# Attention of a fused attention, expert and feed-forward kernel: order from a list scheduler, scores by row halves, V stationary by column halves

## The chip, the cores and the metric

One core of a Trainium2 chip runs the whole program. Each core has five engines with queues of their own, worked off in order: TensorE (matmuls and transposes), VectorE, ScalarE, GpSimd and SyncE, which here issues DMA transfers. The metric is the device time of one execution in microseconds (us), lower is better.

## What is computed

Three layers follow one another; the change is in the first and in the gate of the second. All data are fp32.

```python
# attention: q, k, v are (2, 8, 768, 64), n_global = 8, n_local = 96
rel = pos[:, None] - pos[None, :]
keep = (pos[None, :] < n_global) | ((rel >= 0) & (rel < n_local))
scores = q @ k.T / sqrt(64) - slopes[h] * dist      # dist: |rel|, n_local for far global keys
a = softmax(where(keep, scores, -1e9)); x = a @ v   # x: 1536 tokens of 512
# experts: 8 of them, 512 -> 1024 -> 512, capacity 384
expert = argmax(x @ w_gate); gate_w = softmax(x @ w_gate)[expert]
y = gate_w * (relu(x @ w1[expert]) @ w2[expert])
# feed-forward: 512 -> 2048 -> 512
out = softplus(y @ w_in) @ w_out
```

## The kernel before

`fast_path` works through three stages. **Attention** has 12 tiles: 2 batches with 6 blocks of 128 queries. A query sees its own block of 128 keys, the 96 keys before it and 8 global keys, so a full tile has 232 columns of scores per head, and the first block of a batch (tiles 0 and 6) has 128. **The experts** take the tokens sorted by expert, **the feed-forward layer** takes them in three chunks of 512 and 16 blocks of the hidden layer, 48 steps, each with a first and a second group of products. Both of these keep the weights as a high and a low part, and so take three products where attention takes one.

Order is set by the program text: the framework is told to keep the order in which the instructions are written, and adds the waits. Attention is a loop over n = 0 to 103 (L978), where n is the tile times 8 plus the head. Step n issues the exponential of head n-2 (`expo`, L751), the biased scores of head n-1 (`biased`, L740), the scores of head n (`scores`, L731), the transposes of the probabilities of head n-4 (`transp`, L755) and, at every other n, the products with V of heads n-7 and n-6 (`pv`, L774). Preparation of the next tile (`prep`, L680, transposes q and k), loads, and the routing of the tile before (`route`, L809) are hung on chosen heads.

In `scores` the contraction is over 64 channels, but the matmul uses all 128 rows: k is kept with two heads stacked, and q in two zero-padded copies, `qpad`, of which each has one of the two heads. In `pv` the transposed probabilities are the weights (128 columns) and V moves (64 columns and a column of ones, whose product is the sum of the probabilities). `pv` then divides by the sum (L794 to L796). `route` transposes the tokens x in step 0 (L815), multiplies by the gate's weights and finds the expert in step 1 (L823 to L834), and in step 2 takes the gate's probability, the token's rank in its expert, its slot, the weighted token `xg` (on GpSimd, L864) and scatters it to `xs_d` (L805).

Expert 0 doesn't wait for the last two tiles' scatters: `first_base` (L944) multiplies the rows that are already in `xs_d` by the identity, and `first_add` (L954) adds those of the last two tiles by a selection matrix `here`. Beside attention, `conv_step` (L502) turns pieces of w_in and w_out from double to single precision for the last stage, with one piece a call (64 in all), and goes on later; `pump` (L458) loads weights and splits them into parts (L436, L448) once the pieces of a block are converted. `bank` hands out the eight banks of PSUM by four tags: A has 2, B 3, C 2, D 1.

The lines that set the pace in a step of the loop:

```python
nc.tensor.matmul(ps[:, :w], tr[i][h % 2][:, h // 2, :], kwin[t % 2][:, h // 2, c0:], start=True, stop=True)
...
nc.tensor.matmul(ps[:, o:o + D + 1], pT[:w, 2 * (h % 2) + j, :], vsrc[:w, h, :], start=(j == 0), stop=(j == nb - 1))
```

Of the kernel before, what the change touches and what calls it, by code (L numbers as in the profile page):

```python
# [22 lines left out]
P = 128  # L23
# [65 lines left out]
def strict_upper(nc, pool, name, room=None, ints=None, **kw):  # L89

    t = fill_iota(nc, room or pool, [P, P], [[-1, P]], 0, 1, name + "_rel", ints, **kw)
    tri = pool.tile([P, P], BF16, name=name)
    nc.vector.tensor_scalar(tri, t, 0.0, None, op0=ALU.is_lt)
    return tri

# [216 lines left out]
def fast_path(ctx, tc, q, k, v, n_global, n_local, w_gate, w1, w2, cap, w_in, w_out, out, const):  # L312
# [86 lines left out]
    NRAW = 4  # L399
    rawq = deque()  # L400
# [149 lines left out]
    vt = [ac.tile([P, H, D + 1], F32, name=f"vt{i}") for i in range(3)]  # L550
    vp = [ac.tile([P, H, D + 1], F32, name=f"vp{i}") for i in range(2)]
# [19 lines left out]
    def load_v(i):  # L571
        if i >= len(tiles):
            return
        b, t = tiles[i]
        s0 = t * P
        rotated(vt[i % 3][:, :, 0:D], v, b, s0)
# [43 lines left out]
    for t_ in vt + vp:  # L620
        nc.gpsimd.memset(t_[:, :, D:D + 1], 1.0)
    qpad = [[ac.tile([P, H // 2, P], F32, name=f"qpad{i}{j}") for j in range(2)] for i in range(2)]
    for qa, qb in qpad:
        nc.gpsimd.memset(qa[D:], 0.0)
        nc.gpsimd.memset(qb[:D], 0.0)
# [19 lines left out]
    wg = const.tile([P, NC, E], F32, name="wg")  # L645
    nc.sync.dma_start(wg, w_gate.rearrange("(c p) e -> p c e", p=P))
# [21 lines left out]
    def make_bias1(h):  # L668
        if h == 0:
# [8 lines left out]
    tr = {}  # L678

    def prep(i, step):  # L680

        if i >= len(tiles):
            return
        b, t = tiles[i]
        src = ld[i][step].rearrange("p h d -> p (h d)")
        ps = bank("A", "ps_prep")
        for j in range(H // 2):
            nc.tensor.transpose(ps[:, j * P:(j + 1) * P], src[:, j * P:(j + 1) * P], ident)
        psv = ps.rearrange("p (j c) -> p j c", j=H // 2)
        if step == 0:  # L690

            tr[i] = qpad[i % 2]
            nc.vector.tensor_copy(tr[i][0][:D], psv[:D])
            nc.vector.tensor_copy(tr[i][1][D:], psv[D:])
        else:
            nc.scalar.copy(kwin[t % 2][:, :, PRE:], psv)
            del ld[i]

    def prep_first():

        tr[0] = qpad[0]
        for g in range(2):
# [9 lines left out]
            nc.scalar.copy(tr[0][0][:D, js, :], psv[:D, 0])  # L712
            nc.scalar.copy(tr[0][1][D:, js, :], psv[D:, 0])
# [15 lines left out]
    sps, pt_, ptp, pts, pvs, xts = {}, {}, {}, {}, {}, {}  # L729

    def scores(n):  # L731
        i, h = divmod(n, H)
        b, t = tiles[i]
        c0 = 0 if t else PRE
        w = WIN - c0
        ps = bank("B", "ps_s")
        nc.tensor.matmul(ps[:, :w], tr[i][h % 2][:, h // 2, :], kwin[t % 2][:, h // 2, c0:], start=True, stop=True)  # L737
        sps[n] = ps

    def biased(n):  # L740
        i, h = divmod(n, H)
        t = tiles[i][1]
        w = WIN if t else P
        ps = sps.pop(n)
        s_sb = a3.tile([P, WIN], F32, name="s_sb", bufs=5)
        nc.vector.tensor_tensor_reduce(s_sb[:, :w], in0=ps[:, :w], in1=(bias1 if t else bias0)[:, h, :],  # L746
                                       scale=-(D ** -0.5), scalar=3.0e38, op0=ALU.add, op1=ALU.min,
                                       accum_out=negm[:, n:n + 1])
        pt_[n] = s_sb

    def expo(n):  # L751
        w = WIN if tiles[n // H][1] else P
        nc.scalar.activation(pt_[n][:, :w], pt_[n][:, :w], AF.Exp, bias=negm[:, n:n + 1], scale=-1.0)  # L753

    def transp(n):  # L755
        i, h = divmod(n, H)
        nb = 2 if tiles[i][1] else 1
        if h % 2 == 0:
            ptp[n // 2] = bank("C", "ps_pt")
        ps = ptp[n // 2]  # L760
        s_sb = pt_.pop(n)
        o = (h % 2) * 2 * P
        for j in range(nb):
            nc.tensor.transpose(ps[:, o + j * P:o + (j + 1) * P], s_sb[:, j * PRE:j * PRE + P], ident)
        if h % 2:
            ptp.pop(n // 2)
            pT = a3.tile([P, 4, P], F32, name="pT", bufs=2)
            c = nb * P
            src = ps.rearrange("p (a c) -> p a c", a=2)[:, :, :c]
            dst = pT.rearrange("p (a j) c -> p a (j c)", a=2)[:, :, :c]  # L770
            nc.scalar.copy(dst, src)
            pts[n // 2] = pT

    def pv(n):  # L774
        i, h = divmod(n, H)
        b, t = tiles[i]
        nb = 2 if t else 1
        pT = pts[n // 2]
        if h % 4 == 0:
            pvs[n // 4] = bank("D", "ps_pv")  # L780
        ps = pvs[n // 4]
        o = (h % 4) * (D + 1)
        for j in range(nb):
            vsrc, w = (vt[i % 3], P) if j == nb - 1 else (vp[t % 2], PRE)
            nc.tensor.matmul(ps[:, o:o + D + 1], pT[:w, 2 * (h % 2) + j, :], vsrc[:w, h, :], start=(j == 0), stop=(j == nb - 1))
        if h % 2:
            pts.pop(n // 2)
        if h % 4 == 3:
            pvs.pop(n // 4)
            if h == 3:  # L790
                xts[i] = a2.tile([P, H, D], F32, name="x", bufs=3)
            pv_ = ps[:, :4 * (D + 1)].rearrange("p (a d) -> p a d", a=4)
            rs = a2.tile([P, 4], F32, name="rs")
            nc.vector.tensor_scalar(rs, pv_[:, :, D], 1.0e-9, None, op0=ALU.add)  # L794
            nc.vector.reciprocal(rs, rs)
            nc.vector.tensor_tensor(xts[i][:, h - 3:h + 1, :], pv_[:, :, 0:D],  # L796
                                    rs.unsqueeze(2).to_broadcast([P, 4, D]), op=ALU.mult)

    rt = {}
    sc_q = deque()  # L800

    def scatter_x():
        if sc_q:
            sl, xg = sc_q.popleft()
            nc.gpsimd.indirect_dma_start(  # L805
                out=xs_d, out_offset=bass.IndirectOffsetOnAxis(ap=sl, axis=0), in_=xg, in_offset=None,
                bounds_check=NSLOT - 1, oob_is_err=False)

    def route(i, step):  # L809
        x = xts[i]  # L810
        xf = x.rearrange("p h d -> p (h d)")
        if step == 0:
            ps = bank("A", "ps_xT")
            for c in range(NC):
                nc.tensor.transpose(ps[:, c * P:(c + 1) * P], xf[:, c * P:(c + 1) * P], ident)  # L815
            xT = a2.tile([P, NC, P], F32, name="xTr", bufs=1)
            nc.scalar.copy(xT, ps.rearrange("p (c t) -> p c t", c=NC))
            rt[i] = xT
        elif step == 1:
            xT = rt.pop(i)  # L820
            ps = bank("A", "ps_lg")
            for c in range(NC):
                nc.tensor.matmul(ps[:, :E], xT[:, c, :], wg[:, c, :], start=(c == 0), stop=(c == NC - 1))  # L823
            lg = a2.tile([P, E], F32, name="lg")
            nc.vector.tensor_copy(lg, ps[:, :E])
            mx8 = a2.tile([P, 8], F32, name="mx8")
            nc.vector.max(mx8, lg)
            ix8 = a2.tile([P, 8], U32, name="ix8")
            nc.vector.max_index(ix8, mx8, lg)
            nc.vector.tensor_copy(eall[:, i:i + 1], ix8[:, 0:1])  # L830
# [530 lines left out]
```

## Time and profile before

| | |
|---|---|
| median of the runs (598.76, 599.19 and a disturbed one) | 599.19 us |
| the profiled execution, its own time | 600.73 us |
| span of the profiled execution | 598.9 us |
| TensorE busy in the span | 583.5 us (97%), 3446 matmuls |
| VectorE, ScalarE, GpSimd busy | 348.0, 277.9, 107.3 us |
| mean granted clock of TensorE | 0.989 |
| moved by DMA | 91.85 MB, 153 GB/s |

A profile shows one execution. The span runs from its first to its last instruction. An engine is busy while one of its instructions runs; for TensorE the matmuls overlap, so that a row's duration is longer than the distance to the next one's start. In a row of the timeline stand the start, the duration, the engine, the line of the kernel, the operation, the tile written and the tiles read, the shape, and how many instructions the row merges; a bracket at its end tells how long the engine was idle before it and for whom. [...]

### The profile page before, as it was taken

The numbers are of one execution on the slowest core, as the hardware profiler recorded it, in microseconds if no ns is written. First come the engines' busy times: TensorE is split into PE (matmuls) and PEld (weight loads), VectorE is DVE, ScalarE is ACT, GpSimd is POOL, SyncE is SP. The second block draws the span as 40 slices with busy tenths as digits, with TensorE's granted clock in tenths as the row PEclk, the third lists the DMA queues.
The fourth block names the chain that finished last, engine by engine and source line by source line (L and its number), as shares of the span: only waits on it lengthen the run. The fifth ranks groups of instructions, "written<-read, shape, count | busy, mean of one in ns | idle before, by whom it ended". The sixth has DMA issues, their size and how long they took to land. (4 is left out here: it accounts for less than half of the span.)

```text
span 598.9 us, 9968 instructions
## 1 busy us (share of the span) xinstructions
PE 583.5 (97%) x3446; PEld 523.7 (87%) x3446; DVE 348.0 (58%) x1012; ACT 277.9 (46%) x599; POOL 107.3 (18%) x138
## 2 busy tenths in 40 slices
PE   5999999999999999999999999999999999999995
PEld 4899989999999999999999788888888888888874
DVE  7666888865477883313558774555586433432451
ACT  3566676762565653323444544434553333333340
POOL 3213263321000000000235411120052000200201
PEclk9999999996999999999999999999999999999999
DMA  8857578951797888997963465645202000100101
GB/s 161 219 156 193 139 195 225 286 205 37 251 295 227 257 282 304 379 378 240 323 215 99 122 106 99 108 77 149 81 18 90 0 1 1 53 19 0 71 20 56
DMA packets 90815, 91.85 MB, mean 153 GB/s; under 512 B 43189, under 2 KB 61645, under 8 KB 90757
## 3 DMA queue, kind: packets, MB, share of 16 engines
q1 hardware_dynamic: 82117, 73.30, 42.9%
q10 hardware_dynamic: 6336, 11.54, 6.0%
q0 software_dynamic: 2304, 6.30, 2.9%
q8 instruction: 29, 0.48, 0.4%
q14 instruction: 29, 0.24, 0.2%
HBM read 71.71 MB, written 19.41 MB: 152 GB/s over the span
## 5 line engine op out<-in xcount | busy, mean ns | idle before, releaser
L1236 DVE SCALAR_TENSOR_TENSOR sa<-ps_m,sa 128x512 f32<-128x512 f32 x48 | 33.2, 691 | 112.4 <-ACT sa L1235 112.4
L1233 ACT ACTIVATE sa<-ps_m 128x512 f32<-128x512 f32 x48 | 28.7, 598 | 135.6 <-PE ps_m L1126 135.6
L1124 PE MATMUL ps_m<-zh,w1s 128*128 128x512 f32 x192 | 75.3, 392 | 1.2 <-DVE sa L1236 1.1
L1125 PE MATMUL ps_m<-zl,w1s 128*128 128x512 f32 x192 | 74.8, 390 | 0.0
L1124 PE MATMUL ps_o<-w2s,g 128*128 128x512 f32 x192 | 74.8, 390 | 0.0
L1126 PE MATMUL ps_o<-w2s,g 128*128 128x512 f32 x192 | 74.8, 390 | 0.0
L1126 PE MATMUL ps_m<-zh,w1s 128*128 128x512 f32 x192 | 74.7, 389 | 0.0
L1125 PE MATMUL ps_o<-w2s,g 128*128 128x512 f32 x192 | 74.7, 389 | 0.0
L436 POOL TENSOR_TENSOR w1s<-raw,w1s 128x512 fp32r<-128x512 f32 x16 | 23.2, 1469 | 213.7 <-ACT w1s L448 213.7
L753 ACT ACTIVATE s_sb<-s_sb,negm 128x232 f32<-128x232 f32 (+1 forms) x96 | 44.8, 473 | 35.5 <-DVE negm L746 35.2
L1175 PE MATMUL ps_y<-h,w 128*128 128x232 f32 (+4 forms) x320 | 59.1, 328 | 0.0
L1148 PE MATMUL ps_h<-xT,w 128*128 128x232 f32 (+4 forms) x320 | 58.8, 328 | 0.0
L737 PE MATMUL ps_s<-kwin,qpad 128*128 128x232 f32 (+1 forms) x192 | 56.4, 382 | 1.7 <-DVE negm L746 1.7
L1148 PEld LDWEIGHTS ps_h<-xT,w 128*128 128x128 f32 x320 | 52.9, 190 | 0.7 <-ACT xT L1103 0.2
L1175 PEld LDWEIGHTS ps_y<-h,w 128*128 128x128 f32 x320 | 52.3, 190 | 0.5
L1124 PEld LDWEIGHTS ps_m<-zh,w1s 128*128 128x128 f32 x192 | 36.0, 188 | 10.0 <-DVE sa L1236 2.5
L1126 PEld LDWEIGHTS ps_o<-w2s,g 128*128 128x128 f32 x192 | 36.0, 188 | 7.9 <-DVE g L1244 0.4
L1124 PEld LDWEIGHTS ps_o<-w2s,g 128*128 128x128 f32 x192 | 36.1, 188 | 7.8 <-DVE g L1243 0.3
L1126 PEld LDWEIGHTS ps_m<-zh,w1s 128*128 128x128 f32 x192 | 36.1, 188 | 7.5
L1125 PEld LDWEIGHTS ps_m<-zl,w1s 128*128 128x128 f32 x192 | 36.0, 188 | 7.4 <-DVE zl L1183 0.2
L1125 PEld LDWEIGHTS ps_o<-w2s,g 128*128 128x128 f32 x192 | 36.1, 188 | 7.4
L1157 ACT ACTIVATE h<-ps_h 128x232 f32<-128x232 f32 (+4 forms) x40 | 13.3, 332 | 58.9 <-PE ps_h L1148 56.3
(208 smaller groups left out, 1238.9 us busy)
## 6 DMA issues: line engine op xcount, KB each, us to landing
w<-in_moe_w_dram SPq DMA_DIRECT2D x20, 1024.0 KB, 8.9
raw<-in_moe_w_dram SPq DMA_DIRECT2D x24, 512.0 KB, 4.8
cr<-in_moe_w_in_dram ACTq DMA_DIRECT2D x24, 256.0 KB, 4.4
cr<-in_moe_w_out_dram ACTq DMA_DIRECT2D x20, 256.0 KB, 4.6
xs_d<-early SPq DMA_DIRECT2D x18, 256.0 KB, 3.7
wi_d<-ct SPq DMA_DIRECT2D x32, 128.0 KB, 5.4
wo_d<-ct SPq DMA_DIRECT2D x32, 128.0 KB, 4.5
raw<-wi_d SPq DMA_DIRECT2D x8, 512.0 KB, 5.0
```

The lines of the kernel that those rows point to most:

```text
L436: eng.tensor_tensor(lo, raw, f32(hi), op=ALU.subtract)
L737: nc.tensor.matmul(ps[:, :w], tr[i][h % 2][:, h // 2, :], kwin[t % 2][:, h // 2, c0:], start=True, stop=True)
L753: nc.scalar.activation(pt_[n][:, :w], pt_[n][:, :w], AF.Exp, bias=negm[:, n:n + 1], scale=-1.0)
L1124: nc.tensor.matmul(ps, hi_l, hi_r, start=first, stop=False)
L1125: nc.tensor.matmul(ps, hi_l, lo_r, start=False, stop=False)
L1126: nc.tensor.matmul(ps, lo_l, hi_r, start=False, stop=last)
L1148: nc.tensor.matmul(ps, w[:, c, js], x[:, c, :], start=c == 0, stop=c == NC - 1)
L1157: nc.scalar.activation(h[:, :n], ps, AF.Relu)
L1175: nc.tensor.matmul(ys[ui, d], w[:, j, sl], h, start=f == 0, stop=f == NFE - 1)
L1233: nc.scalar.activation(a, ps, AF.Abs)
L1236: nc.vector.scalar_tensor_tensor(a, in0=ps, scalar=0.0, in1=a, op0=ALU.max, op1=ALU.add)
```

## The change

The loop over n goes. Attention's steps become jobs, each with an engine or a choice of two (`either`), a cost, the jobs it comes after, and buffers that it takes and gives back; `arrange` places them one by one, always the one that can start first, and at equal times the one with the smaller rank (its tile plus a number from a table). The steps are then issued in this order. The costs and ranks are constants of the program, and nothing is decided on the chip.

The steps change too. `scores` takes a tile's eight heads as one job, in 64-row matmuls whose neighbours use rows 0 to 63 and 64 to 127 and different banks; `qpad` becomes one `qT`. `expo` sums the probabilities itself. `transp`, the copies of q and k and that of the outputs may be evicted by ScalarE or VectorE. In `pv` V is the weight, on 64 columns, for two heads on columns 0 to 63 and 64 to 127, so the output comes out transposed and undivided. The gate multiplies it as it is by `wg`, spread over 16 columns for each pair of heads, and `choose` divides the 64 products by the heads' sums and adds them up. The tokens are transposed behind the gate (`rows`) and weighted by VectorE (`weighted`), where GpSimd did it before. Conversion has one call in each of tiles 3 to 10, where tiles 5 to 10 had two.

```diff
+def arrange(jobs, sizes, free):
...
+            for e, c in x.cost.items():
+                s = max(t, free[e])
+                key = (max(s, free[e] + SLACK) + (LEAN if e == "DVE" and len(x.cost) > 1 else 0.0), x.rank, s + c)
+                if best is None or key < best[0]:
+                    best = (key, s, e, x)
...
+    "B": -2.6, "C": -1.84, "CH": 10.69, "CL": 12.72, "CNT": 9.95, "CV": -15.21, "DUP": 13.9, "E": -0.74, "FA":
...
+    NS, NPT, NOT = 8, 6, 2
...
-    for qa, qb in qpad:
-        nc.gpsimd.memset(qa[D:], 0.0)
-        nc.gpsimd.memset(qb[:D], 0.0)
+    qT = [ac.tile([P, H // 2, P], F32, name=f"qT{i}") for i in range(2)]
+    wg = const.tile([P, NC, 2 * E], F32, name="wg")
...
+    def place(h):
+        return h // 4 * 2 + h % 2, h // 2 % 2 * (2 * P)
+
+    def scores(i):
...
+        for h in range(H):
+            j, o = place(h)
+            if o == 0:
+                sps[i, j] = bank("ABBB"[j], "ps_s")
+            r = slice(h % 2 * D, (h % 2 + 1) * D)
+            nc.tensor.matmul(sps[i, j][:, o:o + w], qT[i % 2][r, h // 2, :], kwin[t % 2][r, h // 2, c0:],
+                             start=True, stop=True)
...
+        nc.scalar.activation(s_sb, s_sb, AF.Exp, bias=negm[:, n:n + 1], scale=-1.0, accum_out=dens[i][:, h:h + 1])
...
+        for c in range(2 * g, 2 * g + 2):
+            for j in range(nb):
+                vsrc, w = (vt[i % 3], P) if j == nb - 1 else (vp[t % 2], PRE)
+                for a in range(2):
+                    nc.tensor.matmul(pvs[i][a * D:(a + 1) * D, c * P:(c + 1) * P], vsrc[:w, 2 * c + a, :],
+                                     pts[i, 2 * c + a][:w, j, :], start=(j == 0), stop=(j == nb - 1))
+
+    def keep_o(e, i):
+        ots[i] = a2.tile([P, NC, P], F32, name="oT", bufs=NOT)
+        evict(e, ots[i], pvs.pop(i).rearrange("p (c t) -> p c t", c=NC))
...
+        nc.vector.tensor_tensor(lgh, rt.pop((i, "lg"))[:, :H * E].rearrange("p (h e) -> p h e", h=H),
+                                dens[i].unsqueeze(2).to_broadcast([P, H, E]), op=ALU.mult)
+        lg = a2.tile([P, E], F32, name="lg")
+        nc.vector.tensor_reduce(lg, lgh.rearrange("p h e -> p e h"), axis=AX.X, op=ALU.add)
...
+        nc.vector.tensor_tensor(xg, psin.pop(i).rearrange("p (h d) -> p h d", h=H),
+                                dens.pop(i).unsqueeze(2).to_broadcast([P, H, D]), op=ALU.mult)
...
-    for n in range(NH + 8):
-        i, h = divmod(n, H)
-        if 0 <= n - 2 < NH:
-            expo(n - 2)
...
+        job(("S", i), {"PE": 2.0 if t else 1.3}, lambda e, i=i: scores(i),
+            ([("Q", i), ("K", i)] if i else []) + ([("DUP", i - 1)] if t else []),
+            take=[(("A", "B", "B", "B")[j], ("S", i, j), 0.4 * j) for j in range(4)], lag=0.25)
...
+        if 3 <= i < N:
+            job(("CV", i), {"DVE": 1.05}, lambda e: conv_step(1), [("B", i, H - 1)])
...
+    for _, e, x in arrange(jobs, sizes, {"PE": 7.2, "DVE": 7.6, "ACT": 8.0, "POOL": 8.0, "SP": 6.0}):
+        x.run(e)
```

How the change moves instructions is shown at two places of TensorE's queue; lines are those of each kernel's own program, and xN merges equal instructions. The first is the middle of attention, in a full tile. Before, one head's scores (`ps_s`), another's transposes (`ps_pt`) and the products with V (`ps_pv`) alternate; `ps_prep` is k transposed, `ps_rk` the ranks:

```order
L688 MATMUL ps_prep<-ident,kr 128x128 x4
L737 MATMUL ps_s<-kwin_131,qpad_163 128x232
L764 MATMUL ps_pt<-ident,s_sb 128x128 x2
L841 LDWEIGHTS tri
L841 MATMUL ps_rk<-ohb,tri 128x8
L842 LDWEIGHTS ones
L842 MATMUL ps_rk<-acc,ones 128x8
L737 MATMUL ps_s<-kwin_131,qpad_164 128x232
L764 MATMUL ps_pt<-ident,s_sb 128x128 x2
L785 MATMUL ps_pv<-vp_128,pT 128x65
L785 MATMUL ps_pv<-vt_127,pT 128x65
```

After, the same place in a full tile; `ps_x` is the tokens transposed behind the gate, `ps_lg` the gate's products of the tile before:

```order
L797 MATMUL ps_s<-kwin_130,qT_156 128x232 x8
L863 MATMUL ps_lg<-wg,oT 128x16 x4
L919 MATMUL ps_x<-ident,oT 128x128 x4
L849 MATMUL ps_pv<-pT,vp_129 64x128 x2
L849 MATMUL ps_pv<-pT,vt_126 64x128 x2
L849 MATMUL ps_pv<-pT,vp_129 64x128 x2
L849 MATMUL ps_pv<-pT,vt_126 64x128 x2
L830 MATMUL ps_pt<-ident,s_sb 128x128 x8
L748 MATMUL ps_prep<-ident,kr 128x128 x4
L748 MATMUL ps_prep<-ident,qr 128x128 x4
```

The scores of a tile have moved together into one block of eight at its head, the products with V into groups of eight on 64 rows of output, and the transposes between them into larger runs.

The second place is the end of attention. Before, the base of expert 0's tokens (`ps_x` from `xr`) stands behind the ranks of the tile before the last, on either side of the last tile's token transposes:

```order
L841 LDWEIGHTS tri
L841 MATMUL ps_rk<-ohb,tri 128x8
...
L951 MATMUL ps_x_2202<-ident,xr_2092 128x128
L951 MATMUL ps_x_2202<-ident,xr_2092 128x104
...
L815 MATMUL ps_xT<-ident,x 128x128 x4
L951 MATMUL ps_x_2214<-ident,xr_2092 128x128
L951 MATMUL ps_x_2214<-ident,xr_2092 128x104
...
L823 MATMUL ps_lg<-wg,xTr 128x8 x4
```

After, in the same stretch:

```order
L863 MATMUL ps_lg<-wg,oT 128x16 x4
L1015 MATMUL ps_x_2078<-ident,xr_2017 128x128
L1015 MATMUL ps_x_2078<-ident,xr_2017 128x104
...
L889 LDWEIGHTS tri
L889 MATMUL ps_rk<-ohb,tri 128x8
...
L1015 MATMUL ps_x_2088<-ident,xr_2017 128x128
L1015 MATMUL ps_x_2088<-ident,xr_2017 128x104
...
L919 MATMUL ps_x<-ident,oT 128x128 x4
```

The logits (`ps_lg`) and ranks of the last tile have moved: the logits stand ahead of the base, the ranks between its two halves, and the token transposes behind all of it.

## Rows read from the trace of the kernel before

**Rows 1.** The page's engines: busy us (share of the span) xinstructions.

```profile
PE 583.5 (97%) x3446; PEld 523.7 (87%) x3446; DVE 348.0 (58%) x1012; ACT 277.9 (46%) x599; POOL 107.3 (18%) x138
```

**Rows 2.** Stretches: length, PE PEld DVE ACT POOL busy us (xinstructions), clock, DMA, GB/s.

```profile
136.00:145.00 9.00, 9.00 (x41) 8.53 (x42) 4.43 (x36) 2.21 (x7) 0.97 (x1) 0.50 0.08 30
18.90:130.00 111.10, 109.74 (x874) 103.55 (x874) 87.58 (x426) 73.97 (x181) 37.32 (x41) 1.00 0.73 202
```

**Rows 3.** Timeline of TensorE, tile 5 and the start of tile 6.

```profile
58.20 0.56 PE L737 MATMUL ps_s<-kwin,qpad 128*128 128x232 f32 x2
...
61.31 0.96 PE L823 MATMUL ps_lg<-wg,xTr 128*128 128x8 f32 x8
62.13 0.64 PE L737 MATMUL ps_s<-kwin,qpad 128*128 128x232 f32 x2
...
62.82 0.33 PE L785 MATMUL ps_pv<-vp,pT 104*128 104x65 f32 x2
...
63.66 0.61 PE L688 MATMUL ps_prep<-ident,kr 128*128 128x128 f32 x4
64.10 0.56 PE L737 MATMUL ps_s<-kwin,qpad 128*128 128x232 f32 x2
64.50 0.38 PE L764 MATMUL ps_pt<-ident,s_sb 128*128 128x128 f32 x2
64.72 0.17 PE L841 MATMUL ps_rk<-ohb,tri 128*128 128x8 bf16 x1
...
68.86 0.39 PE L737 MATMUL ps_s<-kwin,qpad 128*128 128x128 f32 x2
69.09 0.38 PE L764 MATMUL ps_pt<-ident,s_sb 128*128 128x128 f32 x2
```

**Rows 4.** Timeline of VectorE: start of tile 2, and tile 5.

```profile
26.89 0.40 DVE L746 CUSTOM_DVE_ANT_0 s_sb<-ps_s,bias 128x232 f32<-128x232 f32 x1 [1.28 <-PE ps_s L737]
...
63.02 0.16 DVE L825 COPY lg<-ps_lg 128x8 f32<-128x8 f32 x1
...
64.08 0.39 DVE L746 CUSTOM_DVE_ANT_0 s_sb<-ps_s,bias 128x232 f32<-128x232 f32 x1
...
64.40 0.39 DVE L746 CUSTOM_DVE_ANT_0 s_sb<-ps_s,bias 128x232 f32<-128x232 f32 x1
...
66.92 0.42 DVE L796 TENSOR_TENSOR x<-ps_pv,rs 128x256 f32<-128x256 f32 x1
67.26 0.39 DVE L746 CUSTOM_DVE_ANT_0 s_sb<-ps_s,bias 128x232 f32<-128x232 f32 x1
```

**Rows 5.** Timeline of ScalarE, tile 5.

```profile
64.36 0.59 ACT L696 COPY kwin<-ps_prep 128x512 f32<-128x512 f32 x1 [0.26 <-PE ps_prep L688]
64.84 0.49 ACT L753 ACTIVATE s_sb<-s_sb,negm 128x232 f32<-128x232 f32 x1
65.23 0.29 ACT L839 ACTIVATE lg<-lg,nmx 128x8 f32<-128x8 f32 x1
65.42 0.19 ACT L839 ACTIVATION_READ_ACCUMULATOR lg<-lg,nmx 128x1 f32 x1
65.52 0.47 ACT L753 ACTIVATE s_sb<-s_sb,negm 128x232 f32<-128x232 f32 x1
```

**Rows 6.** Timeline, end of attention: last biased scores, first expert matmul.

```profile
129.72 0.39 DVE L746 CUSTOM_DVE_ANT_0 s_sb<-ps_s,bias 128x232 f32<-128x232 f32 x1
...
147.46 4.97 PE L1148 MATMUL ps_h<-xT,w 128*128 128x232 f32 x24
```

**Rows 7.** Timeline of the last stage, ScalarE and GpSimd, the last weights' split.

```profile
458.43 0.60 ACT L1233 ACTIVATE sa<-ps_m 128x512 f32<-128x512 f32 x1 [3.51 <-PE ps_m L1126]
...
463.87 0.60 ACT L1233 ACTIVATE sa<-ps_m 128x512 f32<-128x512 f32 x1 [2.48 <-PE ps_m L1126]
...
460.95 2.72 POOL L436 TENSOR_TENSOR w1s<-raw,w1s 128x512 fp32r<-128x512 f32 x2 [9.60 <-ACT w1s L448]
```

More of the change, by code (lines that the diff above doesn't have):

```diff
@@ L747, in biased @@
                                        scale=-(D ** -0.5), scalar=3.0e38, op0=ALU.add, op1=ALU.min,
                                        accum_out=negm[:, n:n + 1])
-        pt_[n] = s_sb
+        pt_[i, h] = s_sb
     def expo(n):
[L752 to L756, printed above, removed]
-        nb = 2 if tiles[i][1] else 1
[L758 to L772, printed above, removed]
@@ new lines, in keep_o, with over_den, logits @@
+    def keep_o(e, i):
+        ots[i] = a2.tile([P, NC, P], F32, name="oT", bufs=NOT)
+        evict(e, ots[i], pvs.pop(i).rearrange("p (c t) -> p c t", c=NC))
+    def over_den(i):
+        nc.vector.tensor_scalar(dens[i], dens[i], 1.0e-9, None, op0=ALU.add)
+        nc.vector.reciprocal(dens[i], dens[i])
+    def logits(i):
+        rt[i, "lg"] = ps = bank("A", "ps_lg")
+        for c in range(NC):
+            nc.tensor.matmul(ps[:, c * 2 * E:(c + 1) * 2 * E], ots[i][:, c, :], wg[:, c, :], start=True, stop=True)
@@ new lines, in rows, with weighted, scatter_x @@
+    def rows(i):
+        psin[i] = ps = bank("A", "ps_x")
+        for c in range(NC):
+            nc.tensor.transpose(ps[:, c * P:(c + 1) * P], ots[i][:, c, :], ident)
+    def weighted(i):
+        xg = a2.tile([P, H, D], F32, name="xg", bufs=5)
+        nc.vector.tensor_tensor(xg, psin.pop(i).rearrange("p (h d) -> p h d", h=H),
+                                dens.pop(i).unsqueeze(2).to_broadcast([P, H, D]), op=ALU.mult)
+        rt[i, "xg"] = xg.rearrange("p h d -> p (h d)")
+    def scatter_x(i):
+        xg = rt.pop((i, "xg"))
+        if i >= len(tiles) - 2:
+            moe_x["x", i] = (xg, moe_x.pop(("here", i)))
+        nc.gpsimd.indirect_dma_start(
+            out=xs_d, out_offset=bass.IndirectOffsetOnAxis(ap=rt.pop((i, "sl")), axis=0), in_=xg, in_offset=None,
+            bounds_check=NSLOT - 1, oob_is_err=False)
@@ new lines, in load_first, with start_tri, bias_first, counted @@
+    def load_first():
+        moe_x["xr"] = ac.tile([P, 2, DM], F32, name="xr0")
+        for j, (o, w) in enumerate(spans(FIRST)):
+            nc.sync.dma_start(moe_x["xr"][:w, j, :], xs_d[o:o + w, :])
+    def start_tri():
+        moe_x["tri"] = strict_upper(nc, const, "tri", a2, ints, tag="here")
+    def bias_first(n):
+        make_bias0(ORDER[n])
+        biased(n)
+    def counted():
+        moe_x["routed"] = after_routing(const, *count())
+        next(moe_x["routed"])
+    jobs = []
@@ new lines, in fast_path, with job @@
+    RANK_BY_TILE = set(RANK) - {"ZF", "M1", "FB", "TRI", "XR", "ST", "CNT"}
+    def job(name, cost, run, after=(), **kw):
+        i, *m = name[1:] if name[0] in RANK_BY_TILE else (0, *name[1:2])
+        jobs.append(Job(name, cost, run, [(a if isinstance(a[0], tuple) else (a, 0.0, True)) for a in after],
+                        rank=i + RANK[name[0]] + 0.01 * sum(m), **kw))
+    either = lambda c: {"ACT": c, "DVE": c}
+    n_t = len(tiles)
+    job(("TRI",), {"DVE": 0.5}, lambda e: start_tri(), [("M1", 0)])
```

412 lines of the change are left out of this document (215 added, 197 removed), and 4 rows, old and new, of the table RANK.

## The prediction

> **What bounds the kernel now.** I read the page's table of engines first. TensorE is busy for 97% of the span [rows 1], and busy matmul rows are pipelined, so this says only that little is left between them. Next came the table by stretches: from 18.9 to 130 us, which is attention from its second tile on, TensorE has matmuls in flight for 109.74 of 111.10 us at the full clock, VectorE is busy for 87.58 and ScalarE for 73.97 [rows 2]. So in attention TensorE sets the pace and the two others have slack. The third view, the timeline of TensorE over one tile, says what its time goes to. A row there holds several instructions, so the cost of a step is the distance from its start to the next row's. The first scores of two neighbouring tiles start at 58.20 and 68.86, so a full tile takes 10.66 us [rows 3]. After attention the engine runs without a gap to the end; the experts' first matmul starts at 147.46 [rows 6]. The reader is to see one thing: what shortens attention moves the whole rest forward, as long as the rest finds its weights.
>
> **TensorE, step by step** [rows 3]. [...] One head's scores over 232 columns take 64.50 - 64.10 = 0.40; two transposes take 64.72 - 64.50 = 0.22; the four key-block products of a pair of heads (128-column weights, 65 moving columns) take 63.66 - 62.82 = 0.84; four transposes of q or k take 64.10 - 63.66 = 0.44; the gate's logits take 62.13 - 61.31 = 0.82. A tile before is 8 x 0.40 + 8 x 0.22 + 4 x 0.84 + 2 x 0.44 + 0.44 (x transposed) + 0.82 + 0.05 (ranks) = 10.5, which agrees with 10.66.
>
> After, a tile still has 16 score instructions of 232 columns (two for each matmul in this trace), but on 64 rows each, neighbours on opposite halves. If the halves run side by side, this is 8 x 0.40 / 2 = 1.6. The V products turn round: V is the weight on 64 columns, and 128 columns of probabilities move. A matmul with 128 moving columns takes 69.09 - 68.86 = 0.23 [rows 3], 16 of them 3.6, in pairs on opposite column halves 1.8. The transposes stay (1.76 + 0.88), the token transposes stay in number (0.44), logits 0.82 (16 columns instead of 8, the same weights), ranks 0.05. Sum 7.35.
>
> No row shows two matmuls side by side. The ends are 7.35 (wholly) and 7.35 + 1.6 + 1.8 = 10.75 (not at all). I take 7.35, since the score and V pairs use disjoint rows or columns and disjoint banks.
>
> Each tile also changes the shape of the array six times (into and out of the scores and two V groups). No row prices that either. Two transposes show 0.38 for 0.22 of issue, so one outlasts its issue by 0.16 [rows 3]; I take six such tails, 1.0, with ends 0 and 6 x 0.27 = 1.6, a whole transpose each. TensorE then needs 8.4 us for a full tile. [...]
>
> **VectorE** [rows 4]. Biased scores step by 64.40 - 64.08 = 0.32, eight are 2.6. The gate's choice takes 64.08 - 63.02 = 1.06 before, seven operations of 8 columns or fewer, 0.15 each; its copy of 8 columns becomes a product and a reduction of 64, which I put at 0.35 more (ends 0.1 and 0.6, two steps of the 256-column row), so 1.4. The slots take six such small operations, 0.9. A 256-column operation out of PSUM steps by 67.26 - 66.92 = 0.34, so the weighting of 512 columns is 0.7 and one conversion step (three operations of 256) is 1.0. The denominators add two small ones, 0.3. This is 6.9. The normalisation and the two half copies of q are gone.
>
> **ScalarE** [rows 5]. An exponential steps by 65.23 - 64.84 = 0.39. It now gives the sum, which appears as an accumulator read; that row starts at 65.42 and the next instruction at 65.52, so 0.10 each: 8 x 0.49 = 3.9, gate 0.29, conversion 0.4 (by the exponential's columns): 4.6. A 512-column eviction takes 64.84 - 64.36 = 0.48.
>
> Seven evictions a tile can go to either engine. In the changed order 20 of 82 stand on VectorE. VectorE is then at 6.9 + 1.7 x 0.68 = 8.1 and ScalarE at 4.6 + 5.3 x 0.48 = 7.1.
>
> **The period.** What is late next is the other two engines: 8.4, 8.1 and 7.1 lie close together, their queues are in order, and each waits in the others' results. TensorE's scores of the next tile now stand as one block of eight, which waits for four banks and so for the biased scores of the tile before. Ends are 8.4 (TensorE never waits) and 10.66 (all gained is lost). I take 9.2, a third of the way, because the other engines are left an eighth and a quarter of slack by it, where before they had a fifth and a third [rows 2].
>
> **The sum.** The first biased score of tile 2 starts at 26.89 [rows 4]. Tile 1's two q copies (4 x 0.34 by the row above) leave VectorE ahead of it, and the start is bound by VectorE's bias tables otherwise: 25.9. Tiles 2 to 5 take 4 x 9.2, tile 6 (no previous block; TensorE 5.9 by the same steps) 7.5, tiles 7 to 10 again 4 x 9.2: tile 11's first biased score starts at 107.0. In the changed order choose, slots and one weighting stand between its eight, so the last starts about 5.9 later (2.6 + 1.4 + 0.9 + 0.7 + 0.3), at 112.9. Before it starts at 129.72 [rows 6]: 16.8 earlier.
>
> From there to the experts' first matmul it is 147.46 - 129.72 = 17.7 before. I keep 17.7. Normalisation and the token transposes leave the last tile's chain (two small operations and 0.34, and four transposes with a copy, some 2). But the base of expert 0's tokens now stands ahead of the last ranks on TensorE, and waits for a load that waits for the scatter of tile 9, whose weighting stands just ahead of the last biased score; queued behind it are the ranks, and behind these VectorE's slots and the count. I price this at 2, with ends 0 and 6. [...]
>
> **What comes later.** Attention converts eight pieces of w_in and w_out instead of twelve, so the last weights of the last stage are cast later: in ScalarE's order behind the 29th step's activation instead of the 25th, and the 31st step needs them. Steps are 463.87 - 458.43 = 5.44 apart. Before, the 25th activation starts at 458.43 and GpSimd's low halves end at 460.95 + 2.72 = 463.67 [rows 7], 5.2 later. From the 29th, the 31st step's activation is 10.9 away and its products begin half a step, 2.7, ahead of it, 8.2 later. That is 3 us of cover, and I cost this at nothing; without cover it is up to 5.4. Loads of q, k and v are issued two tiles ahead, some 18 us instead of 21.
>
> So the profiled execution (600.73, span 598.9) becomes 583.9; the median of the runs shown is 599.19, 1.5 below it: **582**.
>
> **Rivals.**
> - *The queues wait for one another.* For it: three engines within 1.3 us. Against it: eight score buffers and six of transposed probabilities. At a period of 10.0 the last biased score starts at 25.9 + 80 + 8 + 5.9 = 119.8, a gain of 10: 589.
> - *The weights of the V halves aren't hidden.* The trace has weight loads under running matmuls everywhere: scores step by 0.40 with two loads inside. If in column halves they weren't, 32 loads at half of the 0.11 step add 1.8: period about 10.5, gain 6, 593. [...]
> - *The halves don't run side by side*, so the change doesn't do what it says on TensorE: 10.75 + 1.0 = 11.75 a tile, last biased score at 25.9 + 94 + 8.5 + 5.9 = 134.3, 4.6 late: 604.
> - *The clock falls in attention* (the other side). Before, TensorE has the full clock while it is never idle, and 0.50 in the sparse stretch behind it [rows 2]. Now it waits for a tenth of the time. [...] In that sparse stretch it had matmuls in flight for 9.00 of 9.00 us, so these alone don't hold the clock. Against it: 111 us of attention, with as many short matmuls, ran at 1.00.
>
> **Chances.** Forecast 0.58 (570 to 588: period 8.4 to 9.6, chain of the end 4 either way), waiting queues 0.14, weights not hidden 0.08, no halves 0.08, clock 0.12. The range to 605 leaves out the clock and little else. A measurement here tells about 2% from no change, 587.2 and 611.2: faster 0.61 (the forecast and a third of the waiting queues), same 0.26, slower 0.13.
>
> **What would show it.** Right: first biased scores of neighbouring full tiles 8.8 to 9.6 apart; eight heads' scores in 1.6 to 2.1; half a tile's V products in 0.9 to 1.3; idle rows on all three engines; clock 1.00 up to the last tile; the experts' first matmul near 130, and no gap behind it. Wrong: scores in 3.2 (halves one after the other); a clock of 0.5 in the middle tiles; an expert stage that starts early but has gaps where the last weights are due; an end chain over 22 us.

## The result and the profile after

| | before | after |
|---|---|---|
| median of the runs | 598.98 us | 588.14 us |
| ratio, 95% interval | | 0.9832 [0.9804, 0.9859] |
| the profiled execution, its span | 600.73, 598.9 us | 588.03, 586.1 us |

The change makes the kernel 1.7% faster, which is inside the 2% that the chances call no change. The forecast was 582 in a range of 570 to 605: the way and the range hold, and the gain, forecast as 17, is 10.8 us. A fourth run of the kernel before, taken with these, moves its median from 599.19 to 598.98; the disturbed run is left out of the ratio. The steps of the sum, in the two profiled executions:

| | before | forecast | after |
|---|---|---|---|
| first biased score of tile 2 | 26.89 | 25.9 | 27.41 |
| first biased score of tile 11 | | 107.0 | 114.53 |
| last biased score | 129.72 | 112.9 | 120.50 |
| from there to the experts' first matmul | 17.7 | 17.7 | 15.8 |
| from the experts' first matmul to the end of the span | 451.4 | 451.4 | 449.8 |

First the page's engines and the table by stretches, the same ones as in [rows 1, 2] and then five short ones (length, then PE, PEld, DVE, ACT and POOL busy with instructions, granted clock, DMA share, GB/s):

```profile
PE 557.9 (95%) x3446; PEld 489.1 (83%) x3446; DVE 341.8 (58%) x998; ACT 275.9 (47%) x682; POOL 89.3 (15%) x123
```

```profile
18.90:130.00 111.10, 99.87 (x943) 83.77 (x942) 83.49 (x436) 77.48 (x271) 22.01 (x32) 0.94 0.70 199
136.00:145.00 9.00, 9.00 (x49) 8.42 (x48) 1.72 (x11) 2.38 (x7) 0.00 (x0) 1.00 0.73 232
...
14.00:22.00 8.00, 5.70 (x26) 4.40 (x28) 2.74 (x17) 3.37 (x13) 0.11 (x1) 0.58 1.21 251
80.00:88.00 8.00, 7.35 (x41) 5.89 (x42) 4.10 (x21) 4.29 (x14) 0.59 (x2) 0.57 0.42 117
41.60:46.00 4.40, 4.36 (x32) 3.66 (x34) 2.98 (x12) 3.65 (x12) 0.61 (x1) 0.61 0.48 181
26.00:40.00 14.00, 13.65 (x142) 11.70 (x140) 12.11 (x64) 9.33 (x35) 1.63 (x3) 1.00 1.00 253
...
125.00:135.00 10.00, 7.71 (x65) 6.59 (x63) 7.71 (x43) 1.37 (x5) 1.09 (x2) 1.00 0.20 71
```

Where TensorE was idle for 1.4 us of 111.1 before, it is now idle for 11.2, and the mean clock there fell from 1.00 to 0.94. So TensorE no longer sets the pace of attention. The other engines don't either by their busy time. The table of waits of ScalarE (total, times, longest) from tile 2's scores to the last tile's says what does:

```profile
ACT s_sb L819 <- DVE xg L923: 19.2, 5, 5.2
ACT s_sb L819 <- DVE negm L807: 2.3, 3, 1.6
```

An exponential (L819) has nothing to read from `xg`, the weighted tokens that VectorE writes for the scatter (L923), and yet waits for it five times. The timelines of ScalarE, VectorE and TensorE show the first of the five, in tile 3:

```profile
34.84 0.50 ACT L819 ACTIVATE s_sb<-s_sb,negm 128x232 f32<-128x232 f32 x1
35.22 0.21 ACT L819 ACTIVATION_READ_ACCUMULATOR s_sb<-s_sb,negm 128x1 f32 x1
38.84 0.49 ACT L819 ACTIVATE s_sb<-s_sb,negm 128x232 f32<-128x232 f32 x1 [3.41 <-DVE xg L923]
```

```profile
38.07 0.68 DVE L923 TENSOR_TENSOR xg<-ps_x,den 128x512 f32<-128x512 f32 x1
```

```profile
39.06 0.60 PE L919 MATMUL ps_x<-ident,oT 128*128 128x128 f32 x4
41.64 0.66 PE L830 MATMUL ps_pt<-ident,s_sb 128*128 128x128 f32 x4 [1.98 <-ACT pT L737]
```

ScalarE stands from 35.4 until the weighting of tile 0 is over at 38.75, TensorE runs out of probabilities 39.7 us into the span, and when it goes on at 41.64 the granted clock is 0.61 on average over the next 4.4 us. The other four waits end at 58.51, 77.40, 89.37 and 99.55.

What the two have in common is `den`, the heads' sums: the first exponential of a tile takes a new buffer for them (three in turn, L817), and the weighting is the last reader. Tile 3 writes where tile 0 is read until its weighting. `arrange` counts the buffers "s", "pT" and "oT" and the banks, but not these. In its own table of planned times exactly five tiles have their first exponential ahead of the weighting three tiles earlier, and they are the five that wait (planned times, not measured ones):

| tile | first exponential planned | weighting of the tile three before |
|---|---|---|
| 3 | 30.28 | 32.84 |
| 5 | 46.74 | 49.52 |
| 7 | 63.38 | 66.77 |
| 8 | 71.18 | 72.40 |
| 9 | 78.98 | 81.71 |

There is a second loss at the start. TensorE's timeline there, and at the end of attention (first expert matmul last, as in [rows 6]):

```profile
10.76 1.06 PE L748 MATMUL ps_prep<-ident,qr 128*128 128x128 f32 x4
16.22 1.09 PE L748 MATMUL ps_prep<-ident,kr 128*128 128x128 f32 x4 [4.40 <-DMA kr<-in_k_dram]
...
20.43 2.61 PE L797 MATMUL ps_s<-kwin,qT 64*128 64x232 f32 x16
26.13 1.84 PE L797 MATMUL ps_s<-kwin,qT 64*128 64x232 f32 x16
...
128.62 1.12 PE L1015 MATMUL ps_x<-ident,xr 128*128 128x128 f32 x8
130.32 0.18 PE L889 MATMUL ps_rk<-ohb,tri 128*128 128x8 bf16 x1 [0.59 <-DVE nmx L879]
...
136.34 4.97 PE L1254 MATMUL ps_h<-xT,w 128*128 128x232 f32 x24
```

Tile 2's k is transposed ahead of tile 1's scores in the new order, and TensorE waits 4.40 us for its load. The clock is 0.58 on average from 14 to 22 us.

### The profile page after: what moved, and what is told of

The parts are those of the page before. It is cut to its first block, busy times and chain, and to the rows that moved or that the text cites. A ratio compares the mean times of both kernels' runs of the same rounds, so it can differ in the third digit from the quotient of the medians.

```text
span 586.1 us, 9980 instructions
## 1 busy us (share of the span) xinstructions
PE 557.9 (95%) x3446; PEld 489.1 (83%) x3446; DVE 341.8 (58%) x998; ACT 275.9 (47%) x682; POOL 89.3 (15%) x123
## 5 line engine op out<-in xcount | busy, mean ns | idle before, releaser
L819 ACT ACTIVATE s_sb<-s_sb,negm 128x232 f32<-128x232 f32 (+1 forms) x96 | 44.7, 468 | 25.4 <-DVE xg L923 19.2
L86 DVE SCALAR_TENSOR_TENSOR ct<-csq,ct 128x256 int32<-128x256 int32 x64 | 33.2, 519 | 12.2 <-ACT csq L82 11.8
```

What stands on the lines that cost most here:

```text
L86: nc.vector.scalar_tensor_tensor(t, in0=u.bitcast(I32), scalar=3, in1=t, op0=ALU.logical_shift_left, op1=ALU.bitwise_or)
L819: nc.scalar.activation(s_sb, s_sb, AF.Exp, bias=negm[:, n:n + 1], scale=-1.0, accum_out=dens[i][:, h:h + 1])
```

## The experiments

Theory A: the uncounted `den` buffers hold ScalarE, and through it TensorE and its clock. Rivals: the wait is one of order between the two engines whatever the buffers (B), or TensorE's own work is late in any case, since the halves don't run side by side as the sum has it (C). Ratios are to the kernel before on the same chip.

**1. Twelve `den` buffers.** The order of instructions is the same on every engine.

```diff
-            dens[i] = a2.tile([P, H], F32, name="den", bufs=3)
+            dens[i] = a2.tile([P, H], F32, name="den", bufs=12)
```

> The changed kernel with 12 buffers for the heads' sums (den) instead of 3, and the same order of instructions. Theory A: ScalarE's five waits behind the weighting (19.2 us) are for one of the three den buffers, which the list scheduler does not count: the first exponential of tile i takes the buffer that the weighting of tile i-3 still reads. Then these waits go, tile 11's scores start at 100 to 105 us instead of 113.14, the clock stays at 1.00 from 24 us on, and the whole is 575 to 580 us. Rival B, the wait is for the order of the two engines in some other way (the exponential waits for whatever VectorE did last): no change, 588. Rival C, the waits go but TensorE is late in any case: 585 to 588.

Measured: 578.32 us, ratio 0.9648 [0.9615, 0.9681], so 1.8 points better than the change alone. The wait behind `xg` is gone from ScalarE's table, and TensorE's timeline shows two full tiles at TensorE's own pace and, later, a wait for a load:

```profile
33.91 1.84 PE L797 MATMUL ps_s<-kwin,qT 64*128 64x232 f32 x16
...
41.64 1.84 PE L797 MATMUL ps_s<-kwin,qT 64*128 64x232 f32 x16
43.41 1.07 PE L863 MATMUL ps_lg<-wg,oT 128*128 128x16 f32 x8
44.32 1.07 PE L830 MATMUL ps_pt<-ident,s_sb 128*128 128x128 f32 x8
45.23 0.60 PE L748 MATMUL ps_prep<-ident,kr 128*128 128x128 f32 x4
...
46.20 0.44 PE L849 MATMUL ps_pv<-pT,vp 104*64 104x128 f32 x4
...
47.23 1.09 PE L830 MATMUL ps_pt<-ident,s_sb 128*128 128x128 f32 x8
...
49.80 1.84 PE L797 MATMUL ps_s<-kwin,qT 64*128 64x232 f32 x16
...
60.52 1.09 PE L748 MATMUL ps_prep<-ident,kr 128*128 128x128 f32 x4 [3.56 <-DMA kr<-in_k_dram]
```

The scores start 7.7 and 8.2 us apart, and TensorE is never idle between. A is right and B falls. Of the 19.2 us that ScalarE waited, 9.3 come back: tile 11's scores start at 103.87 instead of 113.14. The clock doesn't stay at 1.00, as I had expected: it is 0.67 on average from 60 to 70 us, behind the wait in the last row. That wait takes part of the gain: k of tile 8 is late, and SyncE's table of waits says why:

```profile
SPq L1040 <- DMA cr<-in_moe_w_in_dram: 4.9, 1, 4.9
```

SyncE's transfer of zeros to `ids_d` waits for a load of the conversion that ScalarE issued at 49.98, and k of tile 8 is queued behind it. The two share nothing but a completion semaphore. In the changed kernel's trace records the transfers of SyncE and ScalarE use eight of these in common (101 to 108). Each of the 105 that follow another on the same one in the first 140 us has a wait on that semaphore, and of the 71 in the whole span whose predecessor's landing can be dated none goes out ahead of that landing. In run 1 both transfers have 103; in the changed kernel that load has 107 and goes out at 53.61, behind the zeros (52.53), which wait 0.6 us for VectorE. So an edit that moves no instruction changed which semaphore a transfer has.

**2 and 3. Tile 2's preparation behind tile 1's scores**, alone and with twelve buffers.

```diff
+    late = [y for y in plan if y[2].name in (("PK", 2), ("PQ", 2), ("K", 2), ("Q", 2), ("LD", 4))]
+    plan = [y for y in plan if y not in late]
+    at = 1 + next(n for n, y in enumerate(plan) if y[2].name == ("S", 1))
+    for _, e, x in plan[:at] + late + plan[at:]:
```

> The changed kernel with tile 2's q and k transposes and copies (and the loads of tile 4 behind them) moved in the order from ahead of tile 0's second transposes to just behind tile 1's scores. Theory: TensorE's 4.40 us of idle at 11.8 us, a wait for tile 2's k, and the half clock from 14 to 22 us go; tile 2's first biased score starts at 23 to 25.5 instead of 27.41. If nothing behind takes the gain back, 584 to 586; if the den buffers set the pace from tile 3 on, as theory A says, their waits move with it and the gain is the same 2 to 4. Rival: VectorE's bias tables bind the start, and it is 588.

> Both edits, 12 den buffers and tile 2's preparation behind tile 1's scores. Theory A: the two gains add up, 571 to 577 us, with a period of a full tile of 8.0 to 8.8 us and the full clock throughout. If the two hide one another, no better than the better of the two alone.

Measured: 590.48 us, 0.9857 [0.9824, 0.989], and 583.20, 0.9727 [0.9667, 0.9787]. Neither gains: the first is the changed kernel's time within the intervals, the second lies 0.8 points behind the run with twelve buffers, with intervals that just overlap. TensorE's timeline in the first of them:

```profile
15.57 3.06 PE L797 MATMUL ps_s<-kwin,qT 64*128 64x232 f32 x16
...
24.52 0.73 PE L748 MATMUL ps_prep<-ident,kr 128*128 128x128 f32 x4 [2.90 <-DMA kr<-in_k_dram]
...
28.14 0.54 PE L797 MATMUL ps_s<-kwin,qT 64*128 64x232 f32 x2
```

Tile 1's scores come 4.9 us earlier, but k of tile 4 is transposed ahead of tile 2's scores, and its load goes out only after tile 2's buffers are free. Tile 2's scores start at 28.14 instead of 26.13. Both my theory and the named rival were wrong here: not the bias tables but the next load takes the gain back, and tile 2's scores come 2.0 us later.

**4. The scheduler told of the three buffers.**

```diff
-            job(("E", i, m), {"ACT": 0.5 if t else 0.42}, lambda e, n=n: expo(n), [("B", i, m)])
+            job(("E", i, m), {"ACT": 0.5 if t else 0.42}, lambda e, n=n: expo(n), [("B", i, m)] + ([("N", i - 3)] if i >= 3 and m == 0 else []))
```

> The changed kernel with its 3 den buffers, but the scheduler is told: the first exponential of tile i comes after the weighting of tile i-3. The order of the rest is made anew. Theory A: a planned order with three buffers costs little, since the weighting can come earlier; ScalarE's wait behind the weighting is under 5 us in all, and the whole 577 to 583. Rival B: 586 to 590.

Measured: 582.95 us, 0.9724 [0.969, 0.9757], inside A's range. ScalarE's table keeps one such wait:

```profile
ACT s_sb L819 <- DVE xg L923: 3.4, 1, 3.4
```

An order that knows the limit of three gets 1.1 of the 1.8 points that twelve buffers give.

**5 and 6. The halves one after the other in the order**, with twelve buffers: 5 in the products with V, 6 in the scores, whose four banks are then taken ahead of the first matmul.

```diff
-        for c in range(2 * g, 2 * g + 2):
-            for j in range(nb):
...
-                for a in range(2):
+        for a in range(2):
+            for c in range(2 * g, 2 * g + 2):
+                for j in range(nb):
...
```

```diff
-        for h in range(H):
+        for j in range(4):
+            sps[i, j] = bank("ABBB"[j], "ps_s")
+        for h in (0, 2, 4, 6, 1, 3, 5, 7):
...
-            if o == 0:
-                sps[i, j] = bank("ABBB"[j], "ps_s")
```

> The kernel with 12 den buffers, and in the products with V all products on columns 0 to 63 ahead of all on columns 64 to 127, instead of alternating. The work is the same. If neighbours on opposite column halves run side by side, as the sum of the prediction has it, a group of eight products takes about 1.8 us instead of 1.1, a full tile some 1.4 us more where TensorE sets the pace (8.0 becomes 9.4), and the whole is 586 to 594 us. Rival (no halves side by side): the group stays at 1.1, and it is 578.

> The kernel with 12 den buffers, and in the scores the four heads on rows 0 to 63 ahead of the four on rows 64 to 127. If neighbours on opposite row halves run side by side, a tile's eight scores take about 3.2 us instead of 1.77, a full tile 9.4 instead of 8.0, and the whole 586 to 594 us. Rival (not side by side): 1.77 stays, 578.

Measured: 582.39 us, 0.9732 [0.969, 0.9774], and 585.06, 0.9767 [0.9712, 0.9823]: 0.8 and 1.2 points slower than the alternating order, less than expected. A group of eight V products in run 5, a tile's eight scores in run 6, and stretches of 0.40 us with the count of TensorE's matmul instructions that run in them (in brackets; then clock, DMA share, GB/s), three of run 6 and one of the alternating scores in run 1:

```profile
37.45 0.43 PE L849 MATMUL ps_pv<-pT,vp 104*64 104x128 f32 x2
37.71 0.38 PE L849 MATMUL ps_pv<-pT,vt 128*64 128x128 f32 x2
37.94 0.44 PE L849 MATMUL ps_pv<-pT,vp 104*64 104x128 f32 x4
38.16 0.44 PE L849 MATMUL ps_pv<-pT,vt 128*64 128x128 f32 x4
38.43 0.38 PE L849 MATMUL ps_pv<-pT,vp 104*64 104x128 f32 x2
38.65 0.38 PE L849 MATMUL ps_pv<-pT,vt 128*64 128x128 f32 x2
38.97 0.66 PE L830 MATMUL ps_pt<-ident,s_sb 128*128 128x128 f32 x4
```

```profile
34.90 2.73 PE L797 MATMUL ps_s<-kwin,qT 64*128 64x232 f32 x16
37.55 0.62 PE L863 MATMUL ps_lg<-wg,oT 128*128 128x16 f32 x4
```

```profile
35.30:35.70 0.40, 0.40 (x4) 1.00 1.27 286
35.90:36.30 0.40, 0.40 (x7) 1.00 1.11 181
36.75:37.15 0.40, 0.40 (x4) 1.00 1.22 212
...
41.95:42.35 0.40, 0.40 (x8) 1.00 0.21 82
```

In this order the group takes 38.97 - 37.45 = 1.52 us (alternating 47.23 - 46.20 = 1.03, rows above) and the scores 37.55 - 34.90 = 2.65 (alternating 43.41 - 41.64 = 1.77). I expected 1.8 and 3.2, which supposed that the halves would really run one after the other. They don't. The order of run 5 is two, two, two, two for one half and the same for the other; the rows show two, two, four, four, two, two, and a row of four takes as long as a row of two. So the second half starts when the first is half through, and four of its eight instructions run beside the first half's last four. Run 6 shows the same in its counts: 4, then 7, then 4, where the alternating order has 8.

C falls by the alternating order itself. In run 1's single records the scores start in pairs 0.006 us apart, by the order one on each half, and the pairs follow one another at 0.196 us, the distance of two single full-height records before (64.302 - 64.104 = 0.198). V's pairs follow at 0.11, where full-height matmuls of 128 columns follow at 0.23 / 2 [rows 3]. So two halves run side by side at the full pace of each.

**7. The conversion's loads from GpSimd's queue** in place of ScalarE's, with twelve buffers.

```diff
-    conv_q = [nc.scalar]
+    conv_q = [nc.gpsimd]
```

> The kernel with 12 den buffers, and the conversion's loads issued by GpSimd instead of ScalarE during attention. In the run with 12 buffers SyncE stood from 49.1 to 54.4 us behind a load of the conversion, so tile 8's k came late and TensorE waited 3.56 us and then ran at half the clock until 70. Theory: SyncE's transfers and those of ScalarE share a set of eight semaphores, and one that is late holds the other queue; with the loads on another queue the wait goes, and it is 570 to 575 us. Rival: the wait only moves to another transfer, 576 to 581.

Measured: 576.19 us, 0.9633 [0.9596, 0.967], which is in the rival's range, by little. But in attention the theory holds. The stretch, and TensorE's and GpSimd's timelines at the ends of their work:

```profile
24.00:100.00 76.00, 75.34 (x784) 65.53 (x782) 69.65 (x362) 66.50 (x232) 23.71 (x37) 1.00 0.86 239
```

```profile
27.30 1.84 PE L797 MATMUL ps_s<-kwin,qT 64*128 64x232 f32 x16
...
59.38 1.16 PE L797 MATMUL ps_s<-kwin,qT 64*128 64x128 f32 x16
...
121.30 4.97 PE L1254 MATMUL ps_h<-xT,w 128*128 128x232 f32 x24
```

```profile
565.97 0.97 POOL L1389 DMA_INDIRECT out_dram<-o,ids_sb  x1 [3.12 <-DVE o L1384]
```

TensorE has nothing in flight for 0.7 us of 76, at the full clock, tiles 2 to 5 take 32.08 us, 8.0 each, and the experts' first matmul starts at 121.30 instead of 128.54 with twelve buffers alone. Then 3 us are lost behind the last scatter: 574.1 - 566.94 = 7.2 to the end of the span, where the changed kernel has 586.1 - 582.03 = 4.1.

**8. The scheduler told SyncE's real times**, with twelve buffers and ScalarE's loads. The two issues of v cost 1.0 instead of 0.2 likewise, and a piece of zeros 0.5 instead of 0.1.

```diff
-            job(("LD", i), {"SP": 0.2}, lambda e, i=i: load(i), prev("PQ", "PK") if i > 2 else [], lag=5.0)
+            job(("LD", i), {"SP": 1.7}, lambda e, i=i: load(i), prev("PQ", "PK") if i > 2 else [], lag=5.0)
...
-    for _, e, x in arrange(jobs, sizes, {"PE": 7.2, "DVE": 7.6, "ACT": 8.0, "POOL": 8.0, "SP": 6.0}):
+    for _, e, x in arrange(jobs, sizes, {"PE": 7.2, "DVE": 7.6, "ACT": 8.0, "POOL": 8.0, "SP": 11.0}):
```

> The kernel with 12 den buffers, and the scheduler told what the trace shows of SyncE: it is free for the first tile-2 load at 11.0 us instead of 6.0, three issues of q and k take 1.7 instead of 0.2, two of v 1.0, a piece of zeros 0.5. The order is made anew. Theory: TensorE's order then has tile 2's preparation behind tile 1's scores, its waits for k (8.1 us in three places in the run with 12 buffers) fall to under 4, and it is 570 to 576 us. Rival: the loads are late by themselves, at the start as in the run with tile 2's preparation moved by hand, and it is 578 to 585.

Measured: 578.82 us, 0.9673 [0.9634, 0.9712], no better than twelve buffers alone. The start is as expected, tile 3's scores at 30.80 instead of 33.91. It is given back in tile 5, where the new order has TensorE wait for GpSimd's copy of the previous block of V, with a clock of 0.66 on average from 62 to 72 us behind it:

```profile
62.74 0.44 PE L849 MATMUL ps_pv<-pT,vp 104*64 104x128 f32 x4 [3.92 <-POOL vp L645]
```

**9 to 11. Combinations**: four buffers with SyncE issuing the conversion's loads (`conv_q = [nc.sync]`); number 7 and number 8 together, with ScalarE's loads again behind attention; and four buffers with GpSimd's loads in attention and ScalarE's behind it. The edit of the last:

```diff
-            dens[i] = a2.tile([P, H], F32, name="den", bufs=3)
+            dens[i] = a2.tile([P, H], F32, name="den", bufs=4)
...
-    conv_q = [nc.scalar]
+    conv_q = [nc.gpsimd]
...
     routed = moe_x["routed"]
+    conv_q[0] = nc.scalar
```

> 4 den buffers instead of 3, and the conversion's loads issued by SyncE. In the planned order no first exponential of tile i stands ahead of the weighting of tile i-4, so theory A says that one buffer more is enough: ScalarE's wait behind the weighting is 0 as with 12. With the loads in SyncE's own order no transfer waits for another queue's, but each waits there for a free raw buffer: 574 to 579 us, tile 11's scores at 98 to 104 us. Rival: 4 buffers leave part of the 19.2 us, 580 to 585.

> 12 den buffers, the conversion's loads on GpSimd in attention and on ScalarE behind it, and the scheduler told SyncE's times as in the run before. If the gain at the start (tile 3's scores at 30.80 instead of 33.91 us) adds to that of the loads, 570 to 574 us. Rival: the new order waits elsewhere (for the previous block of V, 3.92 us, in the run with these times alone), 575 to 579.

> 4 den buffers, the conversion's loads on GpSimd in attention and on ScalarE behind it. Attention as in the run with GpSimd's loads (first expert matmul at 121.3 us); that run lost some 3 us behind the last matmul (7.1 us from its last scatter's end to the end of the span, 4.1 in the changed kernel). If that belongs to GpSimd's loads behind attention, 572 to 574 us; if to any of GpSimd's loads, 576 again. With 4 buffers instead of 12 theory A expects no difference.

Measured: 574.44 us, 0.9605 [0.9556, 0.9653]; 574.02, 0.9574 [0.9545, 0.9603]; 573.33, 0.956 [0.9528, 0.9593]. The last has the lowest median of all that were run, 2.7 points better than the change; the three intervals overlap. In both runs with four buffers ScalarE's table has no wait behind `xg`, as A has it: the planned times have no exponential ahead of the weighting four tiles earlier. Rows of the last:

```profile
121.30 4.97 PE L1255 MATMUL ps_h<-xT,w 128*128 128x232 f32 x24
```

```profile
565.92 0.97 POOL L1390 DMA_INDIRECT out_dram<-o,ids_sb  x1 [3.10 <-POOLq L1434]
```

The end is 571.6 - 566.89 = 4.7 us behind the last scatter. The difference lies in GpSimd's last DRAIN, an instruction of its sequencer behind the last scatter: it takes 4.21 us in the changed kernel, where GpSimd issues 36 transfers in all, 4.77 in numbers 10 and 11 with ten loads more, 6.92 in number 7 with forty more. The lines of that DRAIN's place in the program, in the changed kernel and in number 7 (the three durations are shortest, median and longest in ns):

```profile
L1462 POOLq DRAIN  x3: 40/113/4213, 581.1 to 585.9; - x3
L1462 POOLq DRAIN  x3: 50/109/6917, 566.3 to 573.8; - x3
```

So the end grows with GpSimd's loads wherever they stand, by 0.06 to 0.07 us each, and thirty of number 7's forty stand behind attention. Number 9, with these loads in SyncE's own order, has no wait of SyncE for `cr` between 40 and 60 us either. Number 10 lies just past its theory's range, and beside number 11 its better start adds nothing: from 24 to 100 us TensorE has nothing in flight for 3.2 us, in number 11 for 0.5. These are waits of about 1 us or less, and none is for the previous block of V, the wait that its rival named, so what takes the better start is not shown.

## Why the prediction was right, and where it was off

- **TensorE's need: right in sum.** Forecast 8.4 a full tile, measured 7.7 and 8.2 where nothing waits (run 1) and 8.0 over four tiles of run 7. That is 0.65 over the 7.35 without the 1.0 for changes of the array's shape. No run shows that 1.0. Of the 0.65, 0.5 lies in three steps: scores 1.77 for 1.6, V 2 x 1.03 for 1.8, logits 44.32 - 43.41 = 0.91 for 0.82. What the ends of the groups cost stands in run 1's single records: the scores' eight pairs at 0.196 make 1.57, and the 0.20 more lies in the first step (0.30) and the last (0.29); a group of V has 0.14 more than its eight pairs. Together this is 0.5 a tile, half of the 1.0. That the changes of shape cause it isn't shown: in run 6 the second half's first step is 0.30 as well, with no change there.
- **Side by side or not: the choice was right, and so was its bound.** I took 1.6 and 1.8 with ends at twice that, and the pairs' pace gives 8 x 0.196 = 1.57 and 16 x 0.11 = 1.8. Runs 5 and 6 don't measure the other end, since half of each group still ran side by side there; by the single records' pace it would be twice as much, as I had it. So the rival at 604 fell by its condition, and its price stays untested.
- **V's weights: hidden.** The rival at 593 put 1.8 on a tile; V is 0.26 over its forecast, and its pairs follow at the pace of full-height matmuls (0.11), so the 32 loads don't show.
- **The period: the step that failed.** I took 9.2, "a third of the way", because three engines lie close together, and gave *the queues wait for one another* 0.14, against it "eight score buffers and six of transposed probabilities". Measured from tile 2's scores to tile 11's, 113.14 - 26.13 = 87.0 for eight full tiles and tile 6; with 7.5 for tile 6 the full tile is 9.9, the rival's 10.0, and its 589 is the measured 588. But the rival's ground was another one. Slack of the engines doesn't explain it: with one more buffer of 8 columns, and the conversion's loads on another queue, the period is 8.0. The list of buffers in my argument was the scheduler's list. The one that mattered stood in the diff, with its `bufs=3`, and the planned order alone would have shown which five tiles it hits.
- **The start: 0.5 later than before instead of 1.0 earlier.** I had VectorE's bias tables bind it and cost the loads at nothing. TensorE waits 4.40 us for tile 2's k. The scheduler has SyncE free at 6.0, and its first load of tile 2 goes out at 10.98. Run 2, which moved this wait, gained nothing, so what the start cost the whole is not shown.
- **The clock: the rival came true in three places.** It had 0.12. The clock was 0.58, 0.61 and 0.57 in three stretches of 8, 4.4 and 8 us, with or behind waits of TensorE of 4.40, 1.98 and 2.00 us; at those values TensorE gives up at most 8 x 0.42 + 4.4 x 0.39 + 8 x 0.43 = 8.5 us, an estimate, less where it was idle or off the path. Pairs of full scores follow at 0.387 in the scores that start at 83.65, with the clock at 0.52, and at 0.196 where it is 1.00. It came back to 1.00 each time, as from 26 to 40, and in run 7 it is 1.00 from 24 to 100.
- **The chain of the end: 1.9 shorter than forecast.** I kept the old length, of which TensorE spent 9 us at a clock of 0.50 [rows 2]; here it is 1.00 from 125 on. How much of the 1.9 the clock gave, and how much the shorter chain, is not shown. The base of expert 0's tokens ahead of the last ranks, priced at 2, costs nothing: its first half ends at 128.62 + 1.12 = 129.74, and TensorE then still waits 0.59 for what the ranks read.
- **The last weights: hidden, as costed.** TensorE has no wait at all behind 148 us, where before it had one of 1.15 (VectorE's half of an activation) and one of 0.28. These make most of the 1.6 us by which the rest is shorter.
- **What was luck.** The last biased score came 7.6 us later than forecast, and the executions only 4.1 (588.03 for 583.9): two stretches that I had kept at their old length gave 1.9 and 1.6 back. Of the signs that I had named, the scores' 1.6 to 2.1 and V's 0.9 to 1.3 came; the spacing of 8.8 to 9.6 (9.9 on average), the full clock throughout and the experts' first matmul near 130 did not (it starts at 136.34). The range holds because it was wide enough for the rival's period.

## What to carry to other kernels

Where an order is made by a program, list every buffer that turns over in the code and hold it against what the scheduler counts; a tile of 8 columns held ScalarE for 19 us. Where a wait's named releaser shares no data with the waiting instruction, look for a buffer (19.2 us here) or a semaphore (4.9 us in run 1) that the two share. A run that is to keep two things apart must be looked at for whether it did: an order by halves still ran half of each group side by side. And when engines come close together, ask first which wait is forced by the order, before spreading a loss over all of them.

## What the hardware showed that was not expected

- TensorE started matmuls of one half ahead of earlier ones of the other in runs 5 and 6, so across the halves its queue was not worked off in order. In run 5, whose order is all of columns 0 to 63 and then all of 64 to 127, four of the second half's eight run beside the first half's last four (rows of four instructions at 37.94 and 38.16). In run 6 the second series of scores starts at 35.79, beside the first one's fifth (35.78), and three of the first follow it (35.98, 36.18, 36.37). So the scores take 2.65 us and not 3.2, though each series keeps the pace of 0.196.
- Two halves in turn ran side by side in run 1 at the full-height pace of each: pairs of scores 0.196 us apart (full-height records before 0.198), pairs of V products 0.11 (0.23 / 2).
- In run 1 a transfer held another engine's queue by a completion semaphore alone: 4.9 us of SyncE behind a load that ScalarE issued, and 3.56 us of TensorE behind that. With the loads on GpSimd's queue (number 7) or SyncE's own (number 9) SyncE has no such wait between 40 and 60 us.
- Loads issued by GpSimd go with a longer last DRAIN of its sequencer, and so with a longer end of the program: 4.21 us with 36 transfers of GpSimd, 4.77 with 46 (numbers 10 and 11), 6.92 with 76 (number 7). Why is open.
